# Thirty-one more products of constant tiles at the end of TensorE's work, in a Mamba-2 scan followed by a SwiGLU block

## The chip, the cores and the metric

The kernel runs on one core of a Trainium2 chip. The number that counts is the device time of the program in microseconds, from the first to the last instruction with what lies around them. The kernel before takes 369.05 us, the median of three runs that went from 368.32 to 371.51 us.

A core has five engines with a program each: TensorE (PE in the profile; its weight loads are shown apart as PEld), VectorE (DVE), ScalarE (ACT), GpSimd (POOL) and SyncE (SP, which here issues nearly all transfers). They wait for one another by semaphores only.

## The reference, cut to what matters

Two blocks follow each other. The first is a chunked state-space scan over 768 positions, for 4 sequences of 8 heads, head width 32 and state width 16:

```python
y_intra = np.einsum('bhij,bhjd->bhid', M, xc)
y_inter = np.einsum('bhin,bhnd->bhid', Cc, state) * decay_to_i[:, :, :, None]
y[:, :, sl] = y_intra + y_inter
state = decay_full[:, :, None, None] * state + np.sum(Bx, axis=2)
```

Its output is laid out as 3072 tokens of 256 values and goes through a feed-forward block with 1536 hidden columns, after a division by the root mean square:

```python
xn = x / rms * rms_g
g = xn @ w_gate
silu = g * (1.0 / (1.0 + np.exp(-g)))
val = xn @ w_val
return (silu * val @ w_out).astype(np.float32)
```

## The kernel before, in words

The 3072 tokens are taken in six blocks of 512. Each block has two pairs of 128-row chunks of the scan, and then the feed-forward work: for each of 12 slices of 128 hidden columns a gate and a value product (`gv_split`, line 1150, both into banks called `gv`), a Silu, a product with the gate, and then the product with `w_out` (`product_o`, lines 1197 and 1203, into banks called `o`).

Products in full FP32 are avoided for most of this: an operand is split into a high part and a low part with fewer bits, plus a mixed part, and three products in the format FP32R stand for one in FP32. `high_parts[k]`, `low_parts[k]` and `mixed_parts[k]` hold the three parts of piece k of the weights. They are made once, early in the program, and stay in SBUF to the end. A high part is a tile of 128 partitions by 2 by 256 for most pieces; the low and mixed parts of a piece share one tile (`wp`), 512 columns each.

In the blocks 1 to 4, `product_o` keeps the weights stationary and writes the output transposed, 512 columns at a time (line 1197). In the blocks 0 and 5 it keeps the hidden values stationary and streams 256 columns of weights (line 1203). Block 5 is the last, so the end of TensorE's program is a long run of line 1203's products, and behind them two outputs: `putv.5.0`, a copy of one PSUM bank by VectorE, and `put.5.1`, a copy of the other by ScalarE (line 1233). Each is followed by two transfers of 128 rows to DRAM that SyncE issues (line 1236).

The PSUM banks are eight places of 128 by 512 floats in one ring (`one`, line 102). `bank` takes the place that has been free longest, and `used` gives it back when its last reader has been recorded.

The order of all work is written out by hand: a long string of steps (`order`, line 1357), where `b:OX.5.1.1` stands for "block 5, output product of slice 1, second half" and `b:put.5.1` for the last output. The program walks through it and records the instructions of each step on the engines that do them, so an engine's program is the order of the string. The last steps of it are these:

```python
b:OX.5.5.0 b:putv.5.0 b:OX.5.2.1 b:OX.5.1.1 b:put.5.1
```

Behind the last step, SyncE waits for what is still under way, and all engines meet at a barrier; the profile puts these instructions on line 1515.

Of the kernel before, what the change touches and what calls it, by code (L numbers as in the profile page):

```python
# [50 lines left out]
def kernel(  # L51
# [12 lines left out]
    nc = tc.nc  # L64

    P = 128
# [13 lines left out]
    halves = [slice(0, HC), slice(HC, P)]  # L80
# [32 lines left out]
    def view(place, shape, dtype=FP32):  # L113
        ap = place.tile
        if dtype != FP32:
            ap = ap.bitcast(dtype)
        n = 1
        for w in shape[1:]:
            n *= w
        ap = ap[0:shape[0], 0:n]  # L120
        letters = "abcdef"[0:len(shape) - 1]
        if len(letters) > 1:
            ap = ap.rearrange("p (%s) -> p %s" % (" ".join(letters), " ".join(letters)),
                              **{c: w for c, w in zip(letters[1:], shape[2:])})
        return ap
# [3 lines left out]
    def filled(flat):  # L129
        for k in range(fillers.pop() if fillers else 0):  # L130
            nc.tensor.matmul(out=flat, lhsT=warm[:, 0:P], rhs=warm[:, 0:flat.shape[1]], start=True,
                             stop=True)

    def bank(shape, uses, what):
        b = one.take(uses, what)
        v = view(b, shape)
        if fillers:
            filled(view(b, [P, 256]))
        return b, v
# [106 lines left out]
    high_parts, low_parts, mixed_parts = {}, {}, {}  # L246
# [12 lines left out]
    def functions(name):  # L259

        if loaded[0] != name:
            loaded[0] = name
            if name == "silu":
                nc.scalar.preload_act_table(AF.Silu)
            else:
                nc.scalar.preload_act_table_set("natural_log_exp_and_others")  # L266
# [79 lines left out]
    warm = const.tile([P, 256], BF16, name="warm")  # L346
# [125 lines left out]
    def minus_mid():  # L472
# [26 lines left out]
            out=tmask, in_=hmask.rearrange("p (q t) -> p t q", t=2), axis=AX.X),  # L499
# [543 lines left out]
    def norm_apply(blk, t=None):  # L1043

        rb = ps["r", blk]
        r = view(rb, [P, TB])
        y = view(yts[blk], [P, 2, TB])
        if blk:
            nc.vector.scalar_tensor_tensor(out=y[:, t], in0=y[:, t], scalar=gains[:, t:t + 1],
                                           in1=r, op0=ALU.mult, op1=ALU.mult)  # L1050
            xns[blk] = yts[blk], y
        else:
            place = q4.take(uses_of_x(0), "xn")
            xns[0] = place, view(place, [P, 2, TB])
            nc.vector.tensor_tensor(out=xns[0][1], in0=y,
                                    in1=r.unsqueeze(1).to_broadcast([P, 2, TB]), op=ALU.mult)
            yts[0].used()
        rb.used()
# [32 lines left out]
    def uses_of_x(blk):  # L1091
        return 6 * (3 in modes(blk)) + 2 * modes(blk).count(4)
# [127 lines left out]
    def put(blk, b, copy):  # L1220
# [16 lines left out]
        ob.used()  # L1237
        place.used()

    pl, dv, ac = nc.gpsimd, nc.vector, nc.scalar  # L1240

    def start_decays(p, half):
# [42 lines left out]
    def token_out():  # L1285
# [31 lines left out]
        "fetch": fetch,  # L1317
        "table": lambda: functions("silu"), "exps": lambda: functions("exp"),
        "xn": lambda: norm_apply(0),
    }  # L1320


# [155 lines left out]
        b:put.4.0 b:hL.5.10 b:hLp.5.2 b:hK.5.4 b:hH.5.11 b:hid.5.1 b:OX.5.9.1 b:OX.5.10.1 b:hLp.5.11  # L1478
        b:OX.5.2.0 b:hLp.5.4 b:OX.5.6.1 b:OX.5.10.0 b:hK.5.5 b:OX.5.4.0 b:hHv.5.1 b:hL.5.5 b:hK.5.11
        b:hL.5.1 b:OX.5.11.0 b:hK.5.1 b:OX.5.11.1 b:OX.5.5.1 b:OX.5.4.1 b:exps.5 b:OX.5.1.0  # L1480
        b:OX.5.5.0 b:putv.5.0 b:OX.5.2.1 b:OX.5.1.1 b:put.5.1
    """
    for step in order.split():
        group, _, step = step.partition(":")
        step, _, filler = step.partition("*")
# [34 lines left out]
```

## Time and profile before

| What | Value |
|---|---|
| median of three runs | 369.05 us (368.32 to 371.51) |
| span of the profiled execution, first to last instruction | 367.3 us |
| median less that span | 1.7 us |
| TensorE busy with products | 359.3 us, 98% of the span |
| VectorE, ScalarE, GpSimd busy | 275.8, 203.2 and 74.5 us |
| granted TensorE clock, mean | 0.999 |
| last product of TensorE begins | 363.13 us |
| last copy (ScalarE, line 1233) | 363.53 us, 0.59 us long |
| from 363.43 us to the end of the span | 3.87 us, TensorE without work |

The profile has one execution, and its time is told by its span: nothing in it gives the 1.7 us around the span, which is the distance to the median of other executions. In the rows of the profile a product stands as output, arrow, moving operand and weights; "128\*128" is the part of the array that it uses (rows by columns), "128x512" the size of what streams through. FP32R products are printed as f32. The mean duration of a product is longer than the distance between the starts of two neighbours, because products are pipelined: the distance is what a product costs in a row of them.

### The profile page before, as it was taken

What the parts mean: (1) busy time and instruction counts of PE and PEld (TensorE: products, weight loads), DVE (VectorE), ACT (ScalarE), POOL (GpSimd) and SP (SyncE); (2) the same over time, 40 slices, a digit from 0 to 9 for tenths busy, and PEclk for the clock granted to TensorE, in tenths of its full rate; (3) what the DMA queues carried; (4) which work ended last, traced back from release to release, by engine and by line L of the source; (5) the groups of instructions that cost most, each with busy time, mean ns of one, the idle gap of its engine ahead of it and who ended that gap; (6) DMA issues with size and microseconds to landing.
All of it is one profiled execution on the core that took longest, in us unless ns stands there. A gap on an engine that the chain in (4) does not pass through costs nothing.

```text
span 367.3 us, 8226 instructions
## 1 busy us (share of the span) xinstructions
PE 359.3 (98%) x3293; PEld 281.6 (77%) x3293; DVE 275.8 (75%) x514; ACT 203.2 (55%) x346; POOL 74.5 (20%) x79
## 2 busy tenths in 40 slices
PE   8999989999999998999999999999999999999995
PEld 5677455887877776777787788877888888888895
DVE  6899889989988799875866996656447595346790
ACT  3899979999649855386237577134630222421310
POOL 4032010112301321352102316100303001131350
PEclk9999999999999999999999999999999999999999
DMA  7989873754652333342114300110010002001011
GB/s 109 201 135 276 230 284 66 188 136 82 98 125 80 109 57 79 102 69 59 37 30 110 102 0 2 30 30 2 7 29 2 0 9 51 0 0 29 2 29 59
DMA packets 94702, 27.95 MB, mean 76 GB/s; under 512 B 77544, under 2 KB 92616, under 8 KB 94664
## 3 DMA queue, kind: packets, MB, share of 16 engines
q1 hardware_dynamic: 92584, 27.30, 31.8%
q8 instruction: 26, 0.43, 0.5%
q10 hardware_dynamic: 2080, 0.13, 0.4%
q14 instruction: 12, 0.10, 0.1%
HBM read 23.68 MB, written 3.74 MB: 75 GB/s over the span
## 4 chain that ended last, share of the span: by engine, by line
PE 96%; DVE 1%; issue 1%; ACT 0%; POOL 0%; POOLq 0%; ACTq 0%
PE gv L1150 48%; PE o L1197 18%; PE o L1203 10%; PE gv L1140 6%; PE y L916 3%; PE gv L1105 2%; PE g L766 2%; PE A L831 1%; PE g L759 1%; PE y L892 1%; PE e L610 1%; PE ms L1012 0%; PE row L1255 0%; PE y L882 0%; PE e L596 0%
## 5 line engine op out<-in xcount | busy, mean ns | idle before, releaser
L272 ACT ACTIVATE hx<-gv 128x512 f32<-128x512 f32 x70 | 40.4, 597 | 92.1 <-PE gv L1150 48.2
L1150 PE MATMUL gv<-xh,wh 128*128 128x512 f32 x256 | 82.9, 405 | 0.0
L1150 PE MATMUL gv<-xl,wp 128*128 128x512 f32 x256 | 79.2, 390 | 0.0
L1150 PE MATMUL gv<-xk,wp 128*128 128x512 f32 x256 | 79.0, 390 | 0.0
L1078 POOL TENSOR_TENSOR hl<-hx,hh 128x512 fp32r<-128x512 f32 x27 | 40.2, 1498 | 151.3 <-PE o L1197 99.4
L1168 DVE SCALAR_TENSOR_TENSOR hx<-gv,hx 128x512 f32<-128x512 f32 x64 | 43.1, 683 | 28.5 <-PE gv L1150 21.9
L1080 DVE SCALAR_TENSOR_TENSOR hk<-hx,hh 128x512 fp32r<-128x512 f32 x60 | 47.5, 809 | 19.1 <-PE o L1197 14.9
L1150 PEld LDWEIGHTS gv<-xl,wp 128*128 128x128 f32 x256 | 48.1, 188 | 10.4
L1150 PEld LDWEIGHTS gv<-xk,wp 128*128 128x128 f32 x256 | 48.0, 188 | 10.5 <-DVE xk L1080 0.2
L1150 PEld LDWEIGHTS gv<-xh,wh 128*128 128x128 f32 x256 | 46.8, 188 | 10.9 <-issue 1.3
L1197 PE MATMUL o<-hh,wh 128*128 128x512 f32 x96 | 37.9, 395 | 0.0
L1197 PE MATMUL o<-hl,wp 128*128 128x512 f32 x96 | 37.4, 389 | 0.0
L1197 PE MATMUL o<-hk,wp 128*128 128x512 f32 x96 | 37.4, 389 | 0.0
L329 ACT ACTIVATE hh<-hx 128x512 fp32r<-128x512 f32 x35 | 21.6, 626 | 25.3 <-PE o L1197 15.8
L1078 DVE TENSOR_TENSOR hl<-hx,hh 128x512 fp32r<-128x512 f32 x33 | 24.0, 729 | 10.0 <-PE o L1197 7.6
L272 ACT ACTIVATE e<-e,kinks 128x512 f32<-128x512 f32 (+1 forms) x36 | 26.0, 722 | 1.2
L323 DVE SCALAR_TENSOR_TENSOR wp<-wh,w 128x512 fp32r<-128x512 f32 x36 | 25.4, 724 | 0.6 <-ACT wh L329 0.5
L632 POOL TENSOR_SCALAR_AFFINE_SELECT L<-L 64x512 f32<-64x512 f32 (+1 forms) x22 | 17.0, 772 | 34.6 <-ACT L L272 33.8
L1203 PE MATMUL o<-w,hx 128*128 128x256 f32 x96 | 23.0, 381 | 0.0
L1140 PE MATMUL gv<-xn,w 128*128 128x512 f32 x48 | 22.4, 603 | 0.0
L266 ACT ACT_TABLE_LOAD x17 | 21.8, 1283 | 1.1 <-PEq L1504 0.8
L1197 PEld LDWEIGHTS o<-hh,wh 128*128 128x128 f32 x96 | 18.0, 188 | 4.2 <-issue 0.2
(173 smaller groups left out, 523.7 us busy)
## 6 DMA issues: line engine op xcount, KB each, us to landing
L<-rowd SPq DMA_DIRECT2D x32, 128.0 KB
x<-in_x_dram SPq DMA_DIRECT2D x24, 128.0 KB
wr<-in_moe_w_out_dram SPq DMA_DIRECT2D x6, 511.5 KB
wr<-in_moe_w_gate_dram SPq DMA_DIRECT2D x5, 511.5 KB
wr<-in_moe_w_val_dram SPq DMA_DIRECT2D x5, 511.5 KB
out_dram<-ob SPq DMA_DIRECT2D x32, 64.0 KB
bc<-in_B_dram SPq DMA_DIRECT2D x23, 64.0 KB
bc<-in_C_dram SPq DMA_DIRECT2D x23, 64.0 KB
```

The lines of the kernel that those rows point to most:

```text
L266: nc.scalar.preload_act_table_set("natural_log_exp_and_others")
L272: nc.scalar.activation(**operands)
L323: nc.vector.scalar_tensor_tensor(out=(low_parts, mixed_parts)[i][k], in0=high_parts[k], scalar=(-UP, GAIN)[i], in1=view(ws[k], shape), op0 ...
L329: nc.scalar.activation(out=out, in_=in_, func=AF.Copy, scale=scale)
L632: nc.gpsimd.affine_select(out=L[r], in_=L[r], pattern=[[0, L.shape[1]], [1, HC]], compare_op=ALU.is_ge, fill=0.0, base=0, channel_multipli ...
L1078: engine.tensor_tensor(out=out, in0=v, in1=high, op=ALU.subtract)
L1080: nc.vector.scalar_tensor_tensor(out=out, in0=v, scalar=REST, in1=high, op0=ALU.mult, op1=ALU.subtract)
L1140: nc.tensor.matmul(out=o, lhsT=view(ws[k], fetched[k][2])[:, t, f % 2 * P:][:, 0:P], rhs=xn[:, t], start=(t == 0), stop=(t == 1))
L1150: nc.tensor.matmul(out=o, lhsT=weights_of(m, t, f)[part], rhs=view(x, [P, TB], F32R), start=(part == t == 0), stop=(part == 2 and t == 1))
L1168: nc.vector.scalar_tensor_tensor(out=v, in0=o, scalar=GAIN, in1=v, op0=ALU.mult, op1=ALU.mult)
L1197: nc.tensor.matmul(out=o, lhsT=w[:, b * P:(b + 1) * P], rhs=v, start=opens, stop=True, skip_group_check=True)
L1203: nc.tensor.matmul(out=o[:, j * DM:(j + 1) * DM], lhsT=v[:, tk], rhs=w, start=opens, stop=True, skip_group_check=True)
```

## The change

A function `probe` is added with its step, and the step is put into the order between the last product of the last block and the copy of its bank. The step records 31 products. Their operands are tiles that stay unchanged in SBUF since early in the program: as weights the high part of piece 4 (`w`, cut into four tiles of 128 columns), as moving operand the low part of piece 6 (`m`, 512 columns), and for three of them the bfloat16 tile `warm`. Their results go into two PSUM banks that nobody reads.

There are seven forms, in this order:

1. four products with four different weight tiles;
2. four with the same tile;
3. four with the first 96 columns of the four tiles;
4. four with every second column of a 256-column stretch, so that the 128 weight columns lie two floats apart;
5. three with four-byte tiles as in 1 and 384 moving columns;
6. three pairs: one as in 1, and one of `warm` by `warm`, bfloat16, 256 columns;
7. six with 64 rows of weights and of the moving operand, the upper and the lower half of the partitions in turn, each half with its own PSUM bank.

```diff
+    def probe():
+
+        banks = [bank((P, 512), 1, "probe") for k in range(2)]
+        o = [v for b, v in banks]
+        w, m = high_parts[4], low_parts[6].rearrange("p k f -> p (k f)")
+
+        def times(n, lhsT, rhs, out=None, **operands):
+            for k in range(n):
+                nc.tensor.matmul(out=o[0] if out is None else out(k), lhsT=lhsT(k), rhs=rhs(k),
+                                 start=True, stop=True, skip_group_check=True, **operands)
+
+        tiles = [w[:, k // 2, k % 2 * P:k % 2 * P + P] for k in range(4)]
+        times(4, lambda k: tiles[k], lambda k: m)
+        times(4, lambda k: tiles[0], lambda k: m)
+        times(4, lambda k: tiles[k][:, 0:96], lambda k: m, lambda k: o[0][0:96])
+        times(4, lambda k: w[:, k % 2].rearrange("p (c two) -> p two c", two=2)[:, k // 2],
+              lambda k: m)
+        times(3, lambda k: tiles[k], lambda k: m[:, 0:384], lambda k: o[0][:, 0:384])
+        for k in range(3):
+            times(1, lambda _: tiles[k], lambda _: m)
+            times(1, lambda _: warm[:, 0:P], lambda _: warm, lambda _: o[1][:, 0:256])
+        for k in range(6):
+            r = halves[k % 2]
+            times(1, lambda _: tiles[k // 2][r], lambda _: m[r], lambda _: o[k % 2],
+                  tile_position=(r.start, 0))
+        for b, v in banks:
+            b.used()
...
-        b:OX.5.5.0 b:putv.5.0 b:OX.5.2.1 b:OX.5.1.1 b:put.5.1
+        b:OX.5.5.0 b:putv.5.0 b:OX.5.2.1 b:OX.5.1.1 i:probe b:put.5.1
```

On TensorE the end of the program now reads as follows (`wh_1169` is the high part of piece 4, the first `wp` of the new rows the tile with the low part of piece 6; a `+` marks what is new):

```order
 L1203 MATMUL o<-wp,hl 128x256
 L1203 MATMUL o<-wp,hk 128x256
-L1515 UNCONDITIONAL_BRANCH
+L1249 MATMUL probe<-wp,wh_1169 128x512 x8
+L1249 MATMUL probe<-wp,wh_1169 96x512 x4
+L1249 MATMUL probe<-wp,wh_1169 128x512 x4
+L1249 MATMUL probe<-wp,wh_1169 128x384 x3
+L1249 MATMUL probe<-wp,wh_1169 128x512
+L1249 LDWEIGHTS warm
+L1249 MATMUL probe<-warm 128x256
```

All 31 stand behind the last product of line 1203, and none of them carries a wait of its own; the rows left out repeat the pair of forms 6 and end with the six 64-row products. On ScalarE the end is, in the changed kernel, with the waits of its last copy:

```order
298 L272 ACTIVATE hx<-gv 128x512 [waits PE_49]
299 L329 ACTIVATE hh<-hx 128x512 [waits DVE_49] x2
300 L266 ACT_TABLE_LOAD
301 L1233 COPY ob<-o 128x512 [waits PE_49,Activation_49,Pool_49]
302 L1545 UNCONDITIONAL_BRANCH
```

These are the rows that stood there before, but for the line of the branch: the copy waits for the same product of TensorE, the last one of line 1203, which gives its semaphore step ahead of the new products. VectorE, GpSimd and SyncE have no instruction more or less. The program's end has one wait more: SyncE, behind its waits for the last transfers, also waits for the last of the new products before it goes to the barrier of line 1515 (1545 in the changed kernel).

More of the change, by code (lines that the diff above doesn't have):

```diff
@@ L1319 @@
         "xn": lambda: norm_apply(0),
+        "probe": probe,
     }
```

## The prediction

> **What bounds the kernel now.** I read the page's summary first, then the chain that ended last, then the rows of the last microseconds, since the change sits there.
>
> ```profile
> PE 359.3 (98%) x3293; PEld 281.6 (77%) x3293; DVE 275.8 (75%) x514; ACT 203.2 (55%) x346; POOL 74.5 (20%) x79
> ...
> PEclk9999999999999999999999999999999999999999
> ...
> PE 96%; DVE 1%; issue 1%; ACT 0%; POOL 0%; POOLq 0%; ACTq 0%
> ```
>
> TensorE is the bound: busy 98% of the span at full clock, and 96% of the chain that ended last. Whatever is added to its queue ahead of the end is paid, unless something else covers it. What could cover is the way out of the last result, so here are the last pieces of the chain (start, length, what), and then the timeline of the last products, of the last copy and of the transfers that SyncE issues.
>
> ```profile
> 329.10 5.44 PE gv L1150 x24
> ...
> 347.58 15.84 PE o L1203 x132
> 363.43 0.02 issue
> 363.45 0.04 ACTq L1233
> 363.49 0.04 issue
> 363.53 0.59 ACT ob L1233
> ```
>
> ```profile
> 362.80 2.14 SPq L1236 DMA_DIRECT2D out_dram<-ob  x4
> ...
> 363.01 0.28 PE L1203 MATMUL o<-wp,hl 128*128 128x256 f32 x1
> ...
> 363.13 0.28 PE L1203 MATMUL o<-wp,hk 128*128 128x256 f32 x1
> ```
>
> The last product starts at 363.13 and is done at 363.41. ScalarE copies its bank until 364.12 and SyncE has issued the last transfer by 364.94 (362.80 + 2.14). The next rows are SyncE's own waits at the end (line waited for: total us, times, longest), and what the closing line 1515 has on SyncE and on TensorE (duration least, median, most; first and last start).
>
> ```profile
> SPq L1515 <- DMA out_dram<-ob: 1.3, 2, 0.9
> SPq L1515 <- PEq L1515: 0.6, 2, 0.4
> ```
>
> ```profile
> L1515 SPq EVENT_SEMAPHORE  x7: 17/28/28, 365.8 to 367.3; - x7
> ...
> L1515 SPq DRAIN  x3: 7/7/12, 366.6 to 366.9; - x3
> L1515 PEldq DRAIN  x2: 13/1179/2345, 361.1 to 367.0; - x2
> ```
>
> SyncE waits 1.3 us more for the transfers, to about 366.25, goes through its other closing waits until its first drain at 366.6, and the span ends at 367.3. So behind the last product there are 366.25 − 363.41 = **2.8 us in which TensorE has nothing to do**, and then 1.1 us of closing. TensorE's first closing drain began at 361.1 and lasted 2.345 us, to 363.46, just behind the last product: the barrier cannot be passed before TensorE's queue has run empty.
>
> **The change, part by part.** Nothing is removed and nothing moves on the other engines. The last copy still waits for the last product of line 1203, so it and the two transfers behind it run at 363.5 to 366.25 as before, now beside the new products. TensorE gets 31 products with no wait in front (tiles long made, banks long free), so the first starts one step behind 363.13, and the stream runs to its end; then comes the closing. The sum is how long that stream is.
>
> *Forms 1, 2 and 3, twelve products, and form 4 with four.* From the chain: 24 neighbours of the same format and size (FP32R, 128x512) in 5.44 us, 0.227 us each, and 132 of 256 columns in 15.84 us, 0.120 us each. I take 0.227 for each of the sixteen: 16 × 0.227 = 3.63 us. Repeated weights, 96 columns and strided columns change the weight load only, and the load has room:
>
> ```profile
> L1150 PE MATMUL gv<-xl,wp 128*128 128x512 f32 x256 | 79.2, 390 | 0.0
> ...
> L1150 PEld LDWEIGHTS gv<-xl,wp 128*128 128x128 f32 x256 | 48.1, 188 | 10.4
> ```
>
> A load takes 188 ns beside a product that occupies 227, so a shorter or skipped load gains little. The bound below comes from the two widths: 256 more columns cost 0.227 − 0.120 = 0.107 us, so 512 columns alone are 0.214, and 0.013 of each product is not streaming. If all sixteen lost it, that would be −0.2 us. The trace has no strided weights; bounds for form 4 are 0.227 (still hidden) and 0.39 each (a load of twice 188 ns that starts with the product ahead of it, plus 0.013), 0.65 us more for the four. I take hidden, as the nearest row has 39 ns of slack.
>
> *Form 5.* 384 columns lie midway between the two measured widths: (0.227 + 0.120) / 2 = 0.174, three times 0.52 us.
>
> *Form 6.* Three FP32R products at 0.227 and three of bfloat16 with 256 columns. The only pair of such products at a full clock, one behind the other, and its group:
>
> ```profile
> 4.62 0.38 PE L131 MATMUL c<-warm 128*128 128x256 bf16 x2
> ```
>
> ```profile
> L131 PE MATMUL c<-warm 128*128 128x256 bf16 x2 | 0.4, 273 | 0.0
> ```
>
> Two take 0.38 with a duration of 0.273, so the step is 0.11; I take 0.120, as for FP32R of that width. 3 × 0.347 = 1.04 us. A cost of changing the format back and forth isn't in the trace at full clock: bounds nothing and 0.09 us a change (the next row's drain), 0.45 us for the five changes.
>
> *Form 7.* The array goes over from whole rows to halves. What that costs, and whether two halves run side by side, is in these rows of a change to small tiles and of 32-row products in pairs:
>
> ```profile
> 244.77 0.62 PE L1150 MATMUL gv<-xk,wp 128*128 128x512 f32 x2
> 245.32 0.49 PE L916 MATMUL y<-T,S 32*64 32x64 f32 x32
> ```
>
> ```profile
> 10.30 0.38 PE L759 MATMUL g<-T 32*128 32x256 f32 x2
> 10.51 0.38 PE L759 MATMUL g<-T 32*128 32x256 f32 x2
> 10.73 0.38 PE L759 MATMUL g<-T 32*128 32x256 f32 x2
> ```
>
> The second of the line 1150 products starts at 244.77 + 0.227 = 245.00, the first small one 0.32 later: 0.09 more than without the change of tiling. And line 759's products, on different row groups and into different banks, stand two in 0.38 us, the duration of one: they run together, and the next two follow after 0.21. The probe's halves also use different rows and banks. I take three pairs at one product's step: the last pair starts 0.09 + 2 × 0.227 = 0.54 behind where it would, against 0.09 + 5 × 0.227 = 1.23 if the six ran in turn.
>
> *The sum.* First new product 363.13 + 0.12 = 363.25. The last one starts 3.63 + 0.52 + 1.04 + 0.54 = 5.73 later, at 368.98, and is done after 0.39 at 369.37. Then the closing: SyncE's wait for it stands late among its closing waits, so of the closing no less than the 0.7 us from the first drain is left and no more than the 1.1 us from the last landing; I take 0.9. End of span 370.3 against 367.3: **+2.9 us**, and with it 369.05 + 2.9 = **372.0 us**, 0.8% more. The sum stands against the profiled span; the 1.7 us by which the median of the runs is longer than it are taken as unchanged. Of 6.1 us of new stream and its last product, 2.8 lie under the way out and 0.2 to 0.4 of the closing also go under it.
>
> *A rule that speaks against this sum.* The chain's row above has 0.227 us for a product of 512 columns. The Trainium skill, "TensorE: Matmul & The Clock Gate", section "Back-to-back issue gap", says that in a stream of loads and products the spacing is about 131 ns for 512 columns. By that the stream would be about 3.5 us, an estimate, nearly all under the way out, and the time about 369.7. The 24 neighbours at 0.227 speak against it for FP32R operands; I give it no chance apart from the rival below with the same result.
>
> **The rivals.**
>
> *The new products cost nothing* (about 369 us): the end doesn't wait for a result that nobody reads, so the span ends with the transfers as before. For it: no engine reads the two banks. Against it: TensorE's drain of 2.345 us lasted until its last product was done, and SyncE's 0.6 us of waiting for TensorE's queue is part of the closing. It decides only if the stream ends before about 366.3, or if nothing waits. 3 in 100.
>
> *The halves run in turn* (372.7): form 7 costs 1.23 instead of 0.54, +0.7. For it: the trace has no FP32R product on part of the rows, and none with 64 rows and 512 columns; against it: the pairs of line 759. 12 in 100.
>
> *The strided weights aren't hidden* (372.6, and more if a load takes longer than twice): +0.65 for the four. For it: no row shows such a load; against it: nothing but the slack of 39 ns, which a load a fifth longer uses up. 15 in 100.
>
> *Changes of format drain the array* (372.4): +0.45 in form 6. For it: the 0.09 of a change of tiling; against it: nothing direct. 8 in 100.
>
> **How the numbers follow.** The forecast, 372.0, has 62 in 100. Its own range is 371.0 to 372.8: the closing ±0.2, the streaming bound −0.2, and about 0.6 for the median of the runs, which themselves spread from 368.32 to 371.51. Two of the three dear rivals together give 373.1 to 373.4, so the range to be given goes up to 373.9 and down to 371.0; the case of no cost is left out. A difference of about 1%, 3.7 us, is what a measurement of this kernel can tell from none. The forecast lies 0.8 us below that mark, the dear rivals singly at it or just under it, together above it. So slower by over 1%: 0.11 from the forecast's spread, half of the three rivals' 0.35, 0.28 in all, and I say 0.29. Faster by over 1%: no mechanism, 0.01. Within 1%: 0.70.
>
> **What the profile after would show.** Seven forms on the probe's line: sixteen products with 0.227 us between starts, three with 0.174, three pairs with 0.35, then a gap of 0.2 and three pairs with two starts together. The first at 363.25, the last done at 369.4. The last copy still at 363.5 and the last landing at 366.25, now long before the end. A last wait of SyncE for TensorE, and the span ending 0.7 to 1.1 us behind the last product. The forecast is wrong if one form has another step (the strided one above all), if the 64-row products start one by one, or if the work ahead of 363 us, which the change doesn't touch, runs at another time.

## The result, and the profile after

The changed kernel takes 372.29 us (median of 15 runs, 369.01 to 374.31) against 369.34 us for the kernel before in the same comparison (15 runs, 367.53 to 371.51): a ratio of 1.008, with a 95% interval from 1.0053 to 1.0106. That is 2.95 us more, and 372.0 had been forecast. The profiled execution took 371.83 us with a span of 370.1, so the 1.7 us around the span are what they were. Eight of the fifteen runs kept a granted clock of 1.0 and have a median of 371.59 us, seven had 0.995 and 373.23; the clocks of the fifteen of before are not all known, so a part of the 2.95 may be that.

The page's busy times and its summary of the chain that ended last, and then the chain's last pieces (start, length, what):

```profile
PE 365.2 (99%) x3324; PEld 286.1 (77%) x3324; DVE 276.3 (75%) x514; ACT 203.1 (55%) x346; POOL 73.8 (20%) x79
...
PE 97%; DVE 1%; issue 1%; POOL 0%; ACT 0%; POOLq 0%
```

```profile
343.08 4.11 PE gv L1150 x18
347.19 15.83 PE o L1203 x132
363.02 6.20 PE probe L1249 x31
```

TensorE is busy 365.2 us instead of 359.3. The chain ended with the ScalarE copy before; now it ends with the probe, 6.20 us. (A piece of the chain counts from the end of the piece ahead of it, so the stream's first start lies a little earlier.) The timeline of the changed kernel's end, with the copy and with the transfers that SyncE issues:

```profile
362.74 0.28 PE L1203 MATMUL o<-wp,hk 128*128 128x256 f32 x1
...
362.80 1.75 SPq L1236 DMA_DIRECT2D out_dram<-ob  x3
362.86 4.62 PE L1249 MATMUL probe<-wp,wh 128*128 128x512 f32 x20
363.14 0.59 ACT L1233 COPY ob<-o 128x512 f32<-128x512 f32 x1 [12.97 <-PE o L1203]
367.32 0.10 PEld L1249 LDWEIGHTS <-warm 128*128 128x128 bf16 x1 [0.22 <-issue]
367.32 0.28 PE L1249 MATMUL probe<-warm 128*128 128x256 bf16 x1
...
367.69 0.28 PE L1249 MATMUL probe<-warm 128*128 128x256 bf16 x1
...
368.04 0.28 PE L1249 MATMUL probe<-warm 128*128 128x256 bf16 x1
...
368.25 0.53 PEld L1249 LDWEIGHTS probe<-wp,wh 64*128 64x128 f32 x6
368.26 0.97 PE L1249 MATMUL probe<-wp,wh 64*128 64x512 f32 x6
```

The last product of line 1203 starts at 362.74 here, 0.39 earlier than in the profiled execution of before; the two programs don't differ ahead of that point, so this is the scatter between executions, and everything below is counted from it. The copy starts 0.40 behind it, as before (363.53 − 363.13). The last probe product is done at 368.26 + 0.97 = 369.23. What SyncE waited for at the end:

```profile
SPq L1545 <- PE probe L1249: 3.2, 1, 3.2
SPq L1545 <- DMA out_dram<-ob: 1.2, 2, 0.8
SPq L1545 <- PEq L1545: 0.6, 2, 0.4
```

A wait for the probe, 3.2 us, has come behind the waits for the transfers; those are unchanged (1.2 against 1.3). It ends with the probe at 369.23, so it began at 366.0: that is 3.0 us behind the end of the last product of line 1203 (362.74 + 0.28), and work that is done by then keeps nothing waiting. From 369.23 to the end of the span at 370.1 are 0.9 us.

### The profile page after: what moved, and what is told of

It reads as the page before. It is cut to its first block, busy times and chain, and to the rows that moved or that the text cites. A ratio compares the mean times of both kernels' runs of the same rounds, so it can differ in the third digit from the quotient of the medians.

```text
span 370.1 us, 8289 instructions
## 1 busy us (share of the span) xinstructions
PE 365.2 (99%) x3324; PEld 286.1 (77%) x3324; DVE 276.3 (75%) x514; ACT 203.1 (55%) x346; POOL 73.8 (20%) x79
## 4 chain that ended last, share of the span: by engine, by line
PE 97%; DVE 1%; issue 1%; POOL 0%; ACT 0%; POOLq 0%
PE gv L1150 48%; PE o L1197 18%; PE o L1203 10%; PE gv L1140 6%; PE y L916 3%; PE gv L1105 2%; PE probe L1249 2%; PE g L766 2%; PE A L831 1%; PE g L759 1%; PE y L892 1%; PE e L610 1%; PE ms L1012 0%; PE row L1284 0%; PE y L882 0%
```

## Experiments

What they change is the unread work alone, its amount, its place or its forms. Two ask about the time, three about the cost of a product. Those three ran once each (374.77, 374.72 and 378.74 us) and are read from their traces alone.

### Ten products instead of thirty-one

```diff
         times(4, lambda k: tiles[k], lambda k: m)
         times(4, lambda k: tiles[0], lambda k: m)
-        times(4, lambda k: tiles[k][:, 0:96], lambda k: m, lambda k: o[0][0:96])
-        times(4, lambda k: w[:, k % 2].rearrange("p (c two) -> p two c", two=2)[:, k // 2],
-              lambda k: m)
...
+        times(2, lambda k: tiles[k][:, 0:96], lambda k: m, lambda k: o[0][0:96])
```

> Only the first ten of the 31 products are left (four of form 1, four of form 2, two of form 3). Theory (a product at the end costs only what sticks out behind the way out of the last result): the ten take 10 x 0.23 = 2.3 us of steps, the last is done 0.39 after its start, so TensorE ends some 2.5 us behind the last product of line 1203, and 2.8 us are covered: within 0.3 us of the kernel before, ratio 1.000. Rival (each added product is paid, as TensorE bounds the kernel): +2.3 us, ratio 1.006.

368.96 us (12 runs) against 368.63 (17 runs), ratio 1.0009, interval 0.999 to 1.0028. The chain's last piece and SyncE's last waits in this run:

```profile
362.73 2.31 PE probe L1249 x10
```

```profile
SPq L1535 <- DMA out_dram<-ob: 1.2, 2, 0.8
SPq L1535 <- PEq L1535: 0.6, 2, 0.4
```

Ten products take 2.31 us of TensorE, end at 365.04, and no wait for them appears: the transfers are still the last thing SyncE waits for. The chain names the probe, as the last work of an engine, but the time doesn't contain it. The rival's 1.006 lies outside the interval. So at least the 2.3 us that these ten take are free at the end, although TensorE makes up nearly all of the chain elsewhere (96% before). Where the free time ends wasn't tried in steps; the rows before give 2.8 us, SyncE's wait in the changed kernel 3.0.

### The same products one step earlier

```diff
-        b:OX.5.5.0 b:putv.5.0 b:OX.5.2.1 b:OX.5.1.1 i:probe b:put.5.1
+        b:OX.5.5.0 b:putv.5.0 b:OX.5.2.1 i:probe b:OX.5.1.1 b:put.5.1
```

> The same 31 products, recorded one step earlier, ahead of the last six products of line 1203 instead of behind them. Theory (2.8 us of cover at the end is what made 6.2 us of stream cost 3): ahead of the last products nothing covers, so the whole 6.0 us from first to last start, and a change of tiling back to whole rows of 0.1 to 0.15, come on top: +6.0 to +6.3 us against the kernel before, ratio 1.0165. Rival (the loss is the work itself, wherever it stands): +2.9 us as in the changed kernel, ratio 1.008.

375.29 us (5 runs) against 368.63 (17 runs), ratio 1.019, interval 1.0166 to 1.0214. The chain's end:

```profile
347.43 15.11 PE o L1203 x126
362.54 6.20 PE probe L1249 x31
368.74 0.92 PE o L1203 x6
...
369.76 0.58 ACT ob L1233
```

The stream is the same 6.20 us, but now it stands ahead of the last six products, and the copy that ended at 364.12 before ends at 370.34 in this execution, 6.2 us later. The six take 0.92 against 0.72 (6 × 0.120); the 0.2 more is the change back to whole rows, for which 0.1 to 0.15 had been expected. The expected 1.0165 lies just under the interval's lower end, so it was a little too low. The 6.2 us of the copy and the 6.3 us of the two spans (373.6 − 367.3), 1.017, lie inside the interval. The two medians differ by 6.7 us; the two of the five runs that kept a granted clock of 1.0 took 374.74 and 374.95, 6.1 and 6.3 us above 368.63, so at that clock the times agree with the rows. The rival's 1.008 is out. Having the last six products behind the probe and not ahead of it costs about 3 us (375.29 − 372.29): the cover of 2.8 to 3.0 us is lost, and 0.2 comes on top for the change back.

### The 64-row products on one half of the array

```diff
-            r = halves[k % 2]
+            r = halves[0]
```

> Form 7 with the lower half of the partitions alone: six 64-row products on the same rows of the array, still in two banks in turn. Theory (the halves ran together because they stand on different rows): six starts 0.23 apart, the last start 0.68 us later than in the changed kernel. Rival (two banks are what lets them run together): three pairs as before, no change.

One run, with a profile. The timeline of form 7:

```profile
370.48 1.66 PE L1249 MATMUL probe<-wp,wh 64*128 64x512 f32 x6
```

Six products on the same rows take 1.66 us; on the two halves in turn they took 0.97 (row above), 0.69 less. The banks still alternate, so two banks alone don't let products run together; different rows are needed. Whether two row groups would also run together into one bank wasn't tried.

### Where a load becomes the bound

Fifty-six products in place of the 31, eight of each kind (shown: the kinds that the reading uses):

```diff
...
+        strided = lambda k: w[:, k % 2].rearrange("p (c two) -> p two c", two=2)[:, k // 2 % 2]
+        times(8, lambda k: tiles[k % 4], lambda k: m[:, 0:256], one_bank(256))
+        times(8, lambda k: tiles[0], lambda k: m[:, 0:256], one_bank(256))
+        times(8, strided, lambda k: m[:, 0:256], one_bank(256))
+        times(8, lambda k: tiles[k % 4], lambda k: m[:, 0:128], one_bank(128))
+        times(8, strided, lambda k: m[:, 0:128], one_bank(128))
+        times(8, lambda k: tiles[k % 4][:, 0:96], lambda k: m[:, 0:128], lambda k: o[0][0:96, 0:128])
+        times(8, lambda k: tiles[0], lambda k: m[:, 0:128], one_bank(128))
```

> In place of the seven forms: eight products each of 256 moving columns with four weight tiles, with one tile, with strided weights; then of 128 columns with four tiles, strided, with 96 weight columns, and with one tile. Theory (each product has its own load, hidden while the product streams longer than the load needs): 0.120 at 256 columns in all three; at 128 columns the load is what is left, so the step stays well over 0.107 / 2 + 0.013 = 0.067, near 0.11, and is shorter by a quarter with 96 columns. If a strided load is slower, its step is longer than that of the plain one, most clearly at 128 columns. Rival (a tile that is loaded already isn't loaded again): one tile gives 0.107 at 256 and 0.055 to 0.067 at 128, four tiles more. Rival (the 0.013 over the streaming time is fixed and loads never bind): 0.067 at 128 columns everywhere.

The groups of loads (last: mean ns of one), and pieces of the timeline of the loads, from six windows that each lie within one kind: 256 columns with one tile, 256 strided, 128 with four tiles, 128 strided, 128 with 96 weight columns, 128 with one tile.

```profile
L1249 PEld LDWEIGHTS probe<-wp,wh 128*128 128x128 f32 x48 | 5.8, 193 | 0.0
L1249 PEld LDWEIGHTS probe<-wp,wh 128*96 128x96 f32 x8 | 0.8, 165 | 0.0
```

```profile
366.68 0.91 PEld L1249 LDWEIGHTS probe<-wp,wh 128*128 128x128 f32 x7
367.75 0.68 PEld L1249 LDWEIGHTS probe<-wp,wh 128*128 128x128 f32 x5
368.81 0.53 PEld L1249 LDWEIGHTS probe<-wp,wh 128*128 128x128 f32 x4
369.61 0.67 PEld L1249 LDWEIGHTS probe<-wp,wh 128*128 128x128 f32 x5
370.40 0.68 PEld L1249 LDWEIGHTS probe<-wp,wh 128*96 128x96 f32 x7
371.00 0.86 PEld L1249 LDWEIGHTS probe<-wp,wh 128*128 128x128 f32 x7
```

The step of a kind is the length less one load, by the number of loads less one: (0.91 − 0.19) / 6 = 0.120, (0.68 − 0.19) / 4 = 0.12, (0.53 − 0.19) / 3 = 0.11, (0.67 − 0.19) / 4 = 0.12, (0.68 − 0.165) / 6 = 0.086 and (0.86 − 0.19) / 6 = 0.11. So at 256 columns nothing in the weights matters, 0.120 each. At 128 columns, whose streaming alone would be 0.054 (half of 0.107, an estimate), the load sets the step: 0.11 with 128 weight columns, whether the tile is new or the one already there; 0.086 with 96; and a strided load is slower by some 0.006 to 0.01. A load's length isn't its cost: each lasts 0.19 us, and still they follow one another every 0.11. A tile that is loaded already is loaded again. The rivals fall: neither a skipped load nor 0.067 shows.

### Banks, adding, other tiles, and the formats

Forms 1 to 4 had stepped by 0.231 on average (the first twenty products take 4.62 us in the timeline after; less the last one's 0.40 and three steps of 0.174 that leaves 3.70 for sixteen steps), where 0.227 was forecast. Eight products of each kind again:

```diff
...
+        times(8, lambda k: tiles[k % 4], lambda k: m, lambda k: o[k % 2])
+        added(8, lambda k: tiles[k % 4], lambda k: m)
+        times(8, lambda k: tiles[k % 4], lambda k: (m, m2)[k % 2])
+        times(8, lambda k: out_weights_of(k)[0][:, 0:P], lambda k: m)
+        times(8, lambda k: warm[:, 0:P], lambda k: warm, lambda k: o[1][:, 0:256])
...
+        times(8, lambda k: warm[:, 0:P], lambda k: wide, lambda k: o[1].rearrange("p (a b) -> p a b", a=2))
+        for k in range(6):
+            times(1, lambda _: tiles[k % 4], lambda _: m[:, 0:256], lambda _: o[0][:, 0:256])
+            times(1, lambda _: warm[:, 0:P], lambda _: warm, lambda _: o[1][:, 0:256])
```

> In place of the seven forms, eight products each: FP32R 512 columns as in form 1 but into two banks in turn; the same into one bank, each added to the one before instead of overwriting it; the same with two moving tiles in turn; the same with weights of six different pieces and more (eight different pieces); bfloat16 256 columns; bfloat16 512 columns; and six pairs of FP32R and bfloat16, both 256 columns. Open is why form 1 to 4 stepped by 0.231 on average, where neighbours of the same size step by 0.227 in the kernel's own work. Theory (the weights and the moving columns of the probe come from the same two tiles over and over): 0.231 remains with other banks and with adding, and falls to 0.227 with other moving tiles or other weights. Rival (overwriting one bank costs it): two banks or adding give 0.227. For bfloat16: 0.110 at 256 columns as in the one pair of the kernel, and 0.216 to 0.227 at 512; a rival by which 512 columns in a stream step by 0.131 fails if it is over 0.2. For the pairs of formats: the first alternation in the changed kernel cost 0.360 a pair against 0.227 + 0.120; if each change of format costs 0.007, six pairs of 256 columns take 0.25 each, if it is hidden, 0.24.

The chain has the groups' lengths (line 1256 is the adding kind), and the timeline of the loads has a piece of the first kind, one of the third and fourth, and one each of bfloat16 with 256 and with 512 columns:

```profile
364.78 1.84 PE probe L1249 x8
366.62 1.81 PE probe L1256 x8
```

```profile
364.62 1.35 PEld L1249 LDWEIGHTS probe<-wp,wh 128*128 128x128 f32 x6
368.50 2.91 PEld L1249 LDWEIGHTS probe<-wp,wh 128*128 128x128 f32 x13
372.13 0.43 PEld L1249 LDWEIGHTS <-warm 128*128 128x128 bf16 x4
373.00 1.18 PEld L1249 LDWEIGHTS <-warm 128*128 128x128 bf16 x6
```

The first six loads are (1.35 − 0.19) / 5 = 0.232 apart, although the results go into two banks. From the adding kind on the step is 1.81 / 8 = 0.226, and (2.91 − 0.19) / 12 = 0.227. Adding uses the same weight tiles and the same moving tile as the kind ahead of it, so both theories fall: it isn't the tiles that come again, and it isn't the overwriting of one bank. What the slow steps have in common is their place: they are the first ones behind a stretch of 256-column products. The kernel before has that too, in its chain:

```profile
323.66 4.08 PE gv L1150 x18
...
339.98 0.71 PE o L1203 x6
340.70 1.39 PE gv L1150 x6
...
343.48 4.11 PE gv L1150 x18
```

Six products behind line 1203's take 1.39 us, 1.39 / 6 = 0.232. Eighteen behind line 1203's (343.48) take 4.11, and eighteen behind products of 512 columns (323.66, behind line 1197's) take 4.08, so the change of width costs about 0.03 us once. The last copy and its transfers are 20 us away there, so they aren't the cause either. Why the first few step so is open.

These 0.03 are less than half of the 0.07 by which the sixteen steps were longer. The rest lies in forms 3 and 4. Three loads each of the 96-column and of the strided weights, in the timeline of the changed kernel:

```profile
364.71 0.62 PEld L1249 LDWEIGHTS probe<-wp,wh 128*96 128x96 f32 x3
...
365.63 0.66 PEld L1249 LDWEIGHTS probe<-wp,wh 128*128 128x128 f32 x3
```

With loads of 0.161 and 0.197 us the steps are (0.62 − 0.161) / 2 = 0.23 and (0.66 − 0.197) / 2 = 0.23, not 0.227. Whether that is the weights themselves or the change of form isn't shown: no run has a long stretch of either kind at 512 columns.

For bfloat16 the steps are (0.43 − 0.10) / 3 = 0.11 and (1.18 − 0.10) / 5 = 0.216. The pairs of formats are in these rows of the timeline:

```profile
374.63 0.28 PE L1249 MATMUL probe<-warm 128*128 128x256 bf16 x1
...
375.86 0.28 PE L1249 MATMUL probe<-warm 128*128 128x256 bf16 x1
```

Five pairs lie between them: 1.23 / 5 = 0.246 a pair, against 0.120 + 0.11 = 0.23. So a change of format and back costs about 0.015 us, not a drain of 0.09 each way.

## Why the prediction was right, point by point

- **What bounds.** TensorE, with an end where it has nothing to do: shown by the ten products, which cost nothing that could be measured (1.0009), and by the same 31 one step earlier, which cost their whole length (6.2 us in the chain).
- **Forms 1 to 4.** 3.63 us were forecast, sixteen of 0.227; in the trace after they take 3.70. About 0.03 of the 0.07 is missing because 0.227 was read from the long piece of 24 behind products of the same width; the short piece at 340.70 had 0.232, and the probe stands behind the same kind of products. The other 0.04 are the steps of 0.23 in forms 3 and 4, whose cause is open. The strided weights, the rival with 15 in 100, were hidden but for that: the load is about 0.01 longer, not twice as long.
- **The slack.** That the loads stay hidden came true, but the 39 ns of room were misread. The prediction set a load's length, 188 ns, against the 227 of a product. The kernel before already has loads of 192 ns, one for each product, in line 1203's stream of one product every 0.120 us:

```profile
L1203 PEld LDWEIGHTS o<-wp,hl 128*128 128x128 f32 x48 | 9.2, 192 | 0.1
```

So loads overlap one another, and it isn't the length of one that has to fit under a product. What a load costs is the 0.11 us between neighbours where loads are the bound. At 512 columns that leaves about 0.115 us of room, three times the 39 ns, and a strided load at 0.12 us a step fits in easily.

- **Form 5.** Forecast 0.174. The three loads behind the first product of that form, in the timeline of the changed kernel, are (0.54 − 0.19) / 2 = 0.175 apart:

```profile
366.56 0.54 PEld L1249 LDWEIGHTS probe<-wp,wh 128*128 128x128 f32 x3
```

- **Form 6.** Forecast 0.347 a pair. The rows above give 367.69 − 367.32 = 0.37 and 368.04 − 367.69 = 0.35, so 0.36: 0.01 a pair too little, for the changes of format. The drain at each change, the rival with 8 in 100, is out.
- **Form 7.** Two by two, as forecast; the halves in turn, the rival with 12 in 100, would have cost 0.69 by the run on one half, and 0.7 had been worked out. The change of tiling took 0.10 (368.26 − 368.04, less 0.11 to 0.12 for the bfloat16 product), and 0.09 had been forecast. The three pairs take 0.97 with the last product's own 0.39 to 0.40, so their starts cover 0.57 where 0.45 was forecast, the largest miss of the sum. The first pair behind the change is the slow one, 0.50 us long where a product of this width takes 0.39:

```profile
368.26 0.50 PE L1249 MATMUL probe<-wp,wh 64*128 64x512 f32 x2
```

Its load starts with it (368.25) and not with the product ahead, as the loads of the first forms do; that this is the reason is argued, not shown.

- **The whole stream.** First to last start 5.73 forecast, 5.97 found (362.86 to 368.83, the latter being 369.23 less 0.40): +0.24, which is 0.07 from forms 1 to 4, about 0.04 from form 6 and 0.13 from form 7.
- **The closing.** 0.9 us taken from bounds of 0.7 and 1.1; found 0.9. The nothing-waits rival fell with the 3.2 us that SyncE waits for the probe.
- **The rule.** FP32R steps by 227 to 232 ns at 512 columns and bfloat16, by the last experiment, by 216. By the Trainium skill's page "TensorE: Matmul & The Clock Gate", section "Back-to-back issue gap", 131 ns for 512 columns in a stream would have hidden nearly everything, an estimate. No stream here has that step. The same section of the Trainium skill has N/2.4 + 2.5 ns for the isolated gap at full clock, which gives 215.8 for 512 columns and 109 for 256, estimates. The bfloat16 rows agree with it (216 and 110 in a stream); the FP32R rows are 11 to 16 ns above it.

The stream's end then says what the span should have gained over before, counted from the last product of line 1203: 370.1 − 362.74 = 7.4 against 367.3 − 363.13 = 4.2, so 3.2 us. The medians differ by 2.95, within the interval of 2.0 to 3.9 us. The forecast of 2.9 was 0.3 short of the trace's 3.2, nearly all of it the 0.24 by which the stream was longer. That the medians agree with the forecast to 0.05 us is luck: the terms do so only to 0.3, and the interval is 2 us wide.

## What to carry to other kernels

A busy engine that bounds a kernel can still have free time at its very end, as long as the last result's copy and transfers take: work put behind the last product is free up to that, and the same work one step ahead of it is paid in full. Take the step of a product from neighbours in the same surroundings, not from the longest run of its kind. A product in a row of them costs the longer of two steps, its own and its load's, and a load's step is the distance between neighbouring loads (0.11 us here), not the length of one (0.19): the weights (repeated, 96 columns, strided) made no difference at 256 moving columns and less than 0.01 us a product at 512, and all of it could be seen at 128.

## What the runs showed of the hardware that was not expected

- The first six FP32R products of 512 columns behind a stretch of 256-column ones step by 0.232 us, later ones of the same form by 0.227, in the probe and in the kernel's own work. The cause is open.
- A repeated weight tile is loaded again each time: 0.11 us a step at 128 columns with one tile as with four.
- Loads of 0.19 us overlap one another: they follow every 0.11 us where nothing else holds them, every 0.086 with 96 weight columns.
- FP32R pays about 0.013 us a product over its streaming time, at 512, 384 and 256 columns alike; bfloat16 pays 0.002 to 0.004 (0.216 at 512 columns and 0.11 at 256, so 0.106 for 256 columns more and 0.212 for 512).
- An execution in which the granted clock drops in one slice takes about 2 us longer. In the run with the 64-row products on one half, the page's row of the granted clock has such a slice and the mean is 0.995 (0.005 × 373 = 1.9 us). The last product of line 1203 comes at 364.96 there, 2.2 us later than in the changed kernel's profile (362.74, mean 1.0). That run's row:

```profile
PEclk9999989999999999999999999999999999999999
```

The clock isn't all of the scatter: at 1.0 the changed kernel's runs still went from 369.01 to 372.94. That is why a change of 3 us in 370 needs many runs, and why the terms here are read within one profile and not from the difference of two spans.
